# Experts' loop: order of a unit's three row stores, of the split of w1 and of the last transpositions in small units

## The chip, the cores and the metric

One core of a Trainium2 chip runs the whole program in one launch. The metric is the device time of that launch in microseconds (us), the median of three runs; a profiled execution of the same program gives the trace.

## The reference, cut to what matters

```python
attn = softmax(scale * q @ pool8(k).T) @ pool8(v)      # 8 x 8 heads, 576 x 64
x = attn.transpose(0, 2, 1, 3).reshape(4608, 512)

do = x @ w_skip > 0                       # tokens that go through an expert
e = argmax(x[do] @ w_gate); gate = softmax(x[do] @ w_gate)[e]
x[do] += gate * (relu(x[do] @ w1[e]) @ w2[e])          # 8 experts, 512 -> 1024 -> 512

h = x @ w_in; out = (h * sigmoid(h)) @ w_out           # 512 -> 2048 -> 512
```

The change touches the third stage, the experts. How many tokens an expert gets is known only at run time.

## The kernel before, in words

The program has three stages one after the other: attention (to about 160 us in the trace), the experts (about 160 to 507 us), and the last network. All products are made of three matmuls on split operands (high times high, high times low, low times high), so every operand is split into a high half (ScalarE, a copy to the shorter type) and a low half (VectorE, a subtraction).

**Units.** The tokens after attention lie in DRAM as rows of 520 floats, tensor `xa`: 512 values and 8 logits. Routing has made a table of token numbers by expert. The work is cut into units of up to three tiles of 128 tokens of one expert. The first unit is written out; then a loop, `tc.For_i`, line 1025, runs over the rest but one; the last unit is written out again behind the loop, among work of the next stage. The loop ran ten times here. Each pass reads the unit's number of tokens `n` and its columns of the table from `ut` into registers of every engine, and takes one of three arms: up to 256 rows (small), 320, or 384. 320 is 256 rows and a half tile (`mm2_half`, 64 rows).

**One pass** (lines 1026 to 1046) in the kernel before:

- SP loads the next unit's w1 (`load_w1`, 828, 2 MB in four parts) into `raw1`. `keep` (859) copies this unit's tokens from `xn` to `xr` on ScalarE and VectorE. GpSimd then gathers the next unit's rows from `xa` to `xn` (`gather`, 672, three indirect transfers) and stores tiles 1 and 0 of the unit before from `y` to `xa` (`scatter`, 882, one indirect transfer each).
- `mm1` (863): the first layer, eight blocks of twelve matmuls; each block's result is evicted and split into `hh`, `hl`, and a slice of w2 is split (`w2h`, `w2l`).
- `xtrans` (679) transposes the next unit's tokens on TensorE, two of four 128-column slices at a time, into two PSUM buffers; ScalarE and VectorE split them into `xth`, `xtl`, which the next pass's first layer reads.
- `gates` (891): the gate's weight `gt` from the logits, five small operations on VectorE and an exponential on ScalarE.
- `s2`, `gi`, `si`: small VectorE operations that make the row numbers of tile 2, of the gather after next and of tiles 0 and 1 from the table. In the trace `s2` is named `sq`, as it lies in the same tile.
- `conv1` (841): the split of the next unit's w1, four times; only then may SP load `raw1` again.
- `mm2` (906): the second layer of one tile, 24 matmuls, and a VectorE operation that writes `y` (named `x` in the trace).

In the small arm the order is `mm1`, first transpositions, gates, `s2` (`arm`, 978), then `unit_end` (994): store of tile 2, `gi`, `conv1`, `mm2` of tile 1 (left out when n is at most 128), last transpositions, `mm2` of tile 0, `si`. In the big arms `mm2` of the third tile comes between the first transpositions and `unit_end`.

**What sets the order.** Every engine executes its instructions in the order of the program text: the class `Ordered` records each one, and all have the line of its call, 117. What waits for what follows from the tiles read and written. `xa` is one tensor, so a gather waits for all stores before it, a store for the gather before it and for earlier stores, unless `declare_no_dep` says that two don't touch the same rows. `y`, `gi`, `si` and `s2` have one buffer each. SP runs ahead of the other engines until a load's buffer isn't free.

```python
                self.gather(gi)
                scatter(1)
                scatter(0)
```

Of the kernel before, what the change touches and what calls it, by code (L numbers as in the profile page):

```python
# [37 lines left out]
U = 3  # L38
# [121 lines left out]
class Kern:  # L160
# [686 lines left out]
    def moe(self, xa, up):  # L847
        nc, tc, c = self.nc, self.tc, self.c
        with tc.tile_pool(name="ms", bufs=1) as s1, \
# [13 lines left out]
            def mm1(n, fs=range(8), conv=True):  # L863
                for f in fs:
                    ps = self.hp.tile([P, DM], F32, name=f"hp{f}_{n}", tag="hp")
                    i = 0
                    for w, x in ((self.w1h, xth), (self.w1h, xtl), (self.w1l, xth)):
                        for k in range(4):
                            nc.tensor.matmul(ps[:, 0:n], w[:, k, P * f:P * (f + 1)], x[:, k, 0:n],
                                             start=(i == 0), stop=(i == 11))  # L870
                            i += 1
                    if n == 2 * P + D:
                        self.split(hh[:, f, 0:2 * P], hl[:, f, 0:2 * P], ps[:, 0:2 * P], relu=True)
                        nc.scalar.activation(hx[:, f], ps[:, 2 * P:n], AF.Relu)
                    else:
                        self.split(hh[:, f, 0:n], hl[:, f, 0:n], ps[:, 0:n], relu=True)
                    if conv:
                        self.conv2(raw2, f)
                    else:
                        nc.scalar.copy(self.w2h[:, f], raw2[:, f])  # L880

            def scatter(s, other=None, si=si):

                ids = self.s2 if s == 2 and si is self.si else si[:, s:s + 1]
                ins = nc.gpsimd.indirect_dma_start(xa, bass.IndirectOffsetOnAxis(ap=ids, axis=0), y[:, s],
                                                   None, bounds_check=NT - 1, oob_is_err=False)
                if other:
                    tc.declare_no_dep(ins.ins, other.ins, reason="disjoint rows")
                return ins

            def gates(gt=None):
                L = xr[:, :, DM:XW]
                v = nc.vector
                mx = s2.tile([P, U], F32, name="gmx", tag="gmx")
                v.tensor_reduce(mx, L, AX.X, ALU.max)
                d = s2.tile([P, U, E], F32, name="gd", tag="gd")
                v.tensor_tensor(d, L, bc(mx, 2, E), ALU.subtract)
                nc.scalar.activation(d, d, AF.Exp)
                if gt is None:
                    gt = s2.tile([P, U], F32, name="gt", tag="gt")  # L900
                v.tensor_reduce(gt, d, AX.X, ALU.add)
                v.tensor_scalar(gt, gt, 1e-9, None, ALU.add)
                v.reciprocal(gt, gt)
                return gt

            def mm2(s, gt, between=None):
                ps = (pp if s else self.hp).tile([P, DM], F32, name=f"yp{s}", tag="yp" if s else "hp")
                i = 0
                for f in range(8):
                    if between and f == 4:  # L910
                        between()
                    for h, w in ((hh, self.w2h), (hh, self.w2l), (hl, self.w2h)):
                        nc.tensor.matmul(ps, h[:, f, P * s:P * (s + 1)], w[:, f], start=(i == 0), stop=(i == 23))
                        i += 1
                nc.vector.scalar_tensor_tensor(y[:, s, 0:DM], ps, gt[:, s:s + 1], xr[:, s, 0:DM], ALU.mult, ALU.add)

            def mm2_half(gt):
                ps = pp.tile([P, DM], F32, name="yq", tag="yp")
                for f in range(8):
                    o = D * (f % 2)  # L920
                    nc.tensor.matmul(ps[o:o + D], hx[:, f], raw2[:, f], start=(f < 2), stop=(f >= 6),
                                     skip_group_check=True)
                o = y[0:D, 2, 0:DM]
                nc.scalar.copy(o, ps[D:P])
                nc.vector.tensor_tensor(o, ps[0:D], o, ALU.add)
                nc.vector.scalar_tensor_tensor(o, o, gt[0:D, 2:3], xr[0:D, 2, 0:DM], ALU.mult, ALU.add)
# [34 lines left out]
            def first_unit(cols, nxt):  # L961
                gt = gates()
                nc.vector.tensor_scalar(self.s2, cols[:, U - 1:U], -1.0, None, ALU.add)
                self.ffn_abs(0, self.raw1[:, 0], self.raw1[:, 1])
                for _ in self.ffn_ops(0):
                    pass
                self.ffn_conv3(0)
                self.ffn_load(3)
                self.rows(gi, nxt)
                for s in (2, 1):  # L970
                    mm2(s, gt)
                    if s == 2:
                        scatter(s)
                        nc.vector.tensor_scalar(si[:, 0:U - 1], cols[:, 0:U - 1], -1.0, None, ALU.add)
                self.xtrans((0, 1))
                mm2(0, gt, lambda: self.xtrans((2, 3)))

            def arm(n, e, gt, ld):
                mm1(n)
                if n != 2 * P + D:  # L980
                    load2(e)
                if n == 2 * P:
                    self.xtrans((0, 1))
                gates(gt)
                nc.vector.tensor_scalar(self.s2, self.table[:, bass.ds(ld(3, 0, EMPTY), 1)], -1.0, None, ALU.add)
                if n > 2 * P:
                    if n == 2 * P + D:
                        mm2_half(gt)
                        load2(e)
                    self.xtrans((0, 1))  # L990
                    if n == U * P:
                        mm2(2, gt)

            def unit_end(n, ld, gt, often=False):
                scatter(2)
                cols = self.table[:, bass.ds(ld(1, 0, EMPTY), U - 1)]
                self.rows(gi, ld(1, 2, EMPTY))
                for i in range(4):
                    self.conv1(i)
                if often:  # L1000
                    mm2(1, gt)
                else:
                    with tc.If(n > P) as cmp:
                        nc.before(cmp)
                        mm2(1, gt)
                    nc.after(cmp)
                self.xtrans((2, 3))
                mm2(0, gt)
                nc.vector.tensor_scalar(si[:, 0:U - 1], cols[:, 0:U - 1], -1.0, None, ALU.add)

            entry = lambda i, j, hi, engines: nc.value(self.ut[0:1, i, j:j + 1], hi, engines)
            self.taken()
# [6 lines left out]
            first_unit(self.table[:, SLOTS:EMPTY], entry(1, 1, EMPTY, dve))  # L1019
            for s in (1, 0, 2):  # L1020
                nc.scalar.copy(y[:, s, DM:XW], xr[:, U - 1, DM:XW])
            cols = nc.value(self.qi[0:1, 0:1], EMPTY, dve)
            nc.vector.tensor_scalar(self.sq, self.table[:, bass.ds(cols, U)], -1.0, None, ALU.add)
            nu = nc.values_load(self.nu[0:1, 0:1], min_val=1, max_val=NU - 2)
            with tc.For_i(0, nu, 1, iteration_sync="reg_based") as u:
                ld = lambda i, o, hi: nc.value(self.ut[0:1, i, bass.ds(u + o, 1)], hi)
                e = ld(0, 1, E - 1)
                self.load_w1(e)
                keep()
                n = ld(2, 0, U * P)  # L1030
                self.gather(gi)
                scatter(1)
                scatter(0)
                gt = s2.tile([P, U], F32, name="gt", tag="gt")
                with tc.If(n <= 256) as cmp:
                    arm(256, e, gt, ld)
                    unit_end(n, ld, gt)
                    nc.after(None)
                with cmp.Else():
                    with tc.If(n <= 320) as cmp2:  # L1040
                        arm(320, e, gt, ld)
                    with cmp2.Else():
                        arm(384, e, gt, ld)
                    nc.after(cmp2)
                    unit_end(n, ld, gt, True)
                nc.after(cmp)

            keep()
            scatter(1)
            scatter(0)  # L1050
            b0 = ORDER[0]
            x = self.raw1[:, 0:2].rearrange("p a (b n) -> p (a b) n", n=P)
# [16 lines left out]
            gt = gates()  # L1069
            one = s1.tile([1, 1], F32, name="one", tag="one")  # L1070
            nc.scalar.activation(one, gt[0:1, 0:1], AF.Silu)
            sc = None

            for k in range(5):
                if k < 4:
# [3 lines left out]

            for s in (2, 1):  # L1080
                mm2(s, gt)
                sc = scatter(s, sc, self.sq)
                while done:
                    f = done.pop(0)
                    self.ffn_conv3(f)
                    self.ffn_load(f + 3)
                some(OPS[6 - s])
            mm2(0, gt)
            scatter(0, None, self.sq)
            some(20)  # L1090
            while done:
                f = done.pop(0)
# [831 lines left out]
```

## Time and profile before

| | us |
|---|---|
| three runs | 1238.49, 1238.7, 1235.39 |
| median | 1238.49 |
| profiled execution, its own time | 1240.01 |
| span of its trace | 1238.2 |
| TensorE busy (matmul) | 1194.8, 96% of the span |
| VectorE, ScalarE, GpSimd busy | 937.1, 617.4, 398.1 |
| experts' loop, first unit's first product to the loop's exit | 188.77 to 472.19 |

A window row gives a stretch's length, then the busy time of each engine in it with the number of instructions, TensorE's granted clock (1.00 is 2.4 GHz), the DMA engines' share and their GB/s. A timeline row gives the start, the length, the engine, the instruction with output and inputs, and in brackets the engine's idle time before it with what ended it. "issue" means that the engine waited for nothing that the profile shows. Matmuls overlap, so lengths of single ones add up to more than the time they take.

### The profile page before, as it was taken

How to read it: one execution, taken by the hardware profiler on the slowest of the kernel's cores; microseconds unless marked ns; L12 is line 12 of the kernel's file. 1: busy time of each engine (PE TensorE's matmuls, PEld its weight loads, DVE VectorE, ACT ScalarE, POOL GpSimd, SP SyncE). 2: the span in 40 equal slices, each digit the busy share in tenths (PEclk: the TensorE clock that was granted, in tenths of full speed). 3: DMA queues.
4: the chain of work that ended last, by engine and by line, in shares of the span. 5: the costliest groups of instructions: out<-in, count | busy, mean ns of one | idle time of the engine just before them, and what ended most of it. 6: DMA issues, size and time to landing. Idle time of an engine off the chain costs nothing.

```text
span 1238.2 us, 20329 instructions
## 1 busy us (share of the span) xinstructions
PE 1194.8 (96%) x6173; PEld 1013.6 (82%) x6174; DVE 937.1 (76%) x1572; ACT 617.4 (50%) x1286; POOL 398.1 (32%) x345
## 2 busy tenths in 40 slices
PE   6999898999989999999999999999999999999997
PEld 5988787988878888888888888888888788887885
DVE  5888886566675768989668855767897778977667
ACT  5877534445564555444444334554355543555442
POOL 5477532222232221323357733222112221112210
PEclk9999999999999999999999999999999999999999
DMA  9997537465574753458849783677757786575645
GB/s 373 327 310 269 185 125 280 138 228 177 182 238 139 250 187 89 133 177 245 279 130 321 225 245 112 210 207 210 236 179 228 215 236 230 180 234 184 195 168 144
DMA packets 162767, 260.68 MB, mean 211 GB/s; under 512 B 41669, under 2 KB 91461, under 8 KB 160000
## 3 DMA queue, kind: packets, MB, share of 16 engines
q1 hardware_dynamic: 150880, 241.39, 60.5%
q0 software_dynamic: 7008, 16.80, 4.2%
q10 hardware_dynamic: 4800, 1.51, 0.5%
q8 instruction: 41, 0.67, 0.2%
q14 instruction: 38, 0.31, 0.1%
HBM read 203.16 MB, written 59.18 MB: 212 GB/s over the span
## 4 chain that ended last, share of the span: by engine, by line
PE 53%; DVE 4%; DMA 2%; POOL 1%; issue 1%; ACT 1%; SPq 0%; ACTq 0%; POOLq 0%; DVEq 0%
PE ps L117 17%; PE fopy L117 16%; PE fh L117 9%; PE fop L117 9%; PE yp L117 1%; DMA wout<-wdo 1%; DVE sw L117 1%; POOL sw L117 1%; DVE accc L117 1%; DMA ft<-part 1%; DMA wdi<-fh 0%; DMA wdo<-fl 0%; DVE fr L117 0%; DVE oc L117 0%; DVE c L117 0%
## 5 line engine op out<-in xcount | busy, mean ns | idle before, releaser
L117 PE MATMUL fopy<-c,wout 128*128 128x512 f32 x810 | 192.1, 391 | 2.2 <-DVE accc L117 2.0
L117 PEld LDWEIGHTS fopy<-c,wout 128*128 128x128 f32 x810 | 151.2, 188 | 37.0 <-DVE accc L117 5.0
L117 POOL TENSOR_TENSOR tm<-tm,tm 128x512 f32<-128x512 f32 x24 | 31.8, 1324 | 271.7 <-ACT tm L117 271.7
L117 DVE TENSOR_TENSOR accc<-fopy,accc 128x1024 f32<-128x1024 f32 (+1 forms) x73 | 87.9, 1205 | 23.0 <-PE fopy L117 23.0
L117 ACT ACTIVATE hh<-hp 128x256 fp32r<-128x256 f32 (+1 forms) x96 | 39.4, 410 | 97.7 <-PE hp L117 87.0
L117 DVE TENSOR_TENSOR w2l<-raw,w2h 128x512 fp32r<-128x512 f32 x96 | 65.8, 690 | 28.9 <-ACT w2h L117 26.3
L117 ACT CAST c<-hs 128x512 fp32r<-128x512 f32 x96 | 59.7, 622 | 55.1 <-PE fopy L117 28.0
L117 DVE TENSOR_TENSOR c<-hs,c 128x512 fp32r<-128x512 f32 x96 | 66.0, 688 | 23.6 <-ACT c L117 23.6
L117 POOL TENSOR_TENSOR sw<-sw 128x256 f32<-128x256 f32 x64 | 72.4, 1153 | 35.8 <-DVE sw L117 34.6
L117 PE MATMUL yp<-w2l,hh 128*128 128x512 f32 x208 | 81.7, 393 | 2.0 <-DVE w2l L117 2.0
L117 PE MATMUL yp<-w2h,hh 128*128 128x512 f32 x208 | 83.5, 402 | 0.0
L117 ACT COPY tm<-ps 128x512 f32<-128x512 f32 x72 | 42.0, 583 | 82.9 <-PE ps L117 82.9
L117 PE MATMUL fh<-w1l,fh 128*128 128x512 f32 x336 | 83.0, 389 | 0.0
L117 PE MATMUL yp<-w2h,hl 128*128 128x512 f32 x208 | 81.6, 392 | 0.0
L117 PE MATMUL hp<-xth,w1h 128*128 128x256 f32 (+2 forms) x384 | 72.0, 309 | 6.1 <-issue 2.8
L117 ACT ACTIVATE fsg<-fh 128x512 f32<-128x512 f32 x48 | 28.7, 597 | 92.6 <-PE fh L117 88.3
L117 PE MATMUL hp<-xtl,w1h 128*128 128x256 f32 (+2 forms) x384 | 71.7, 307 | 3.1 <-DVE xtl L117 1.9
L117 PEld LDWEIGHTS fh<-w1l,fh 128*128 128x128 f32 x336 | 63.1, 188 | 13.1
L117 DVE TENSOR_TENSOR fgl<-fsg,fgh 128x512 fp32r<-128x512 f32 x48 | 39.1, 816 | 41.5 <-ACT fgh L117 41.5
L117 ACT ACTIVATE prb<-s,mx 128x72 f32<-128x72 f32 x288 | 65.3, 355 | 10.3 <-DVE mx L117 10.3
L117 PE MATMUL hp<-xth,w1l 128*128 128x256 f32 (+2 forms) x384 | 70.0, 304 | 0.0
L117 PEld LDWEIGHTS hp<-xth,w1h 128*128 128x128 f32 x384 | 59.5, 189 | 9.4 <-issue 6.4
(252 smaller groups left out, 2952.4 us busy)
## 6 DMA issues: line engine op xcount, KB each, us to landing
raw<-w SPq DMA_DIRECT2D x88, 512.0 KB
wout<-wdo SPq DMA_DIRECT2D x135, 256.0 KB
win<-wdi SPq DMA_DIRECT2D x36, 512.0 KB
w1l<-wdi SPq DMA_DIRECT2D x36, 512.0 KB
xa<-x SPq DMA_DIRECT2D x36, 256.0 KB
v<-vR SPq DMA_DIRECT2D x7, 1280.0 KB
w1l<-wdo SPq DMA_DIRECT2D x33, 256.0 KB
fr<-w_in SPq DMA_DIRECT2D x16, 512.0 KB
```

What stands on the lines that cost most here:

```text
L117: ins = f(*a, **k)
```

## The change

- `scatter` takes a list of other stores that it need not wait for. A pass begins with the store of tile 0 alone; the stores of tile 2 and tile 1 both stand in the unit itself and are declared free of the earlier ones of the list. Tile 1's store comes after its `mm2`; a one-element GpSimd copy from `y` to a new tile `seen` stands before it. `si` is made before `mm2` of tile 1 instead of at the end.
- The small arm is a function of its own, `small`: `mm1`, w2's load, first transpositions, `s2`, store of tile 2, `conv1`, gates, `gi`, `si`, `mm2` of tile 1 if n is over 128, copy and store of tile 1, `mm2` of tile 0 with the last transpositions between its first and second half.
- The big arms keep their order but for `si` and the store of tile 1.
- The first unit stores its tile 1 itself; behind the loop one store is left; the last unit's list holds all its earlier stores.

```diff
--- before.py
+++ after.py
@@ -879,13 +879,13 @@
                     else:
                         nc.scalar.copy(self.w2h[:, f], raw2[:, f])
 
-            def scatter(s, other=None, si=si):
+            def scatter(s, others=(), si=si):
 
                 ids = self.s2 if s == 2 and si is self.si else si[:, s:s + 1]
                 ins = nc.gpsimd.indirect_dma_start(xa, bass.IndirectOffsetOnAxis(ap=ids, axis=0), y[:, s],
                                                    None, bounds_check=NT - 1, oob_is_err=False)
-                if other:
-                    tc.declare_no_dep(ins.ins, other.ins, reason="disjoint rows")
+                for o in others:
+                    tc.declare_no_dep(ins.ins, o.ins, reason="disjoint rows")
                 return ins
 
             def gates(gt=None):
@@ -970,43 +970,60 @@
                 for s in (2, 1):
                     mm2(s, gt)
                     if s == 2:
-                        scatter(s)
+                        last = scatter(s)
                         nc.vector.tensor_scalar(si[:, 0:U - 1], cols[:, 0:U - 1], -1.0, None, ALU.add)
+                    else:
+                        scatter(s, [last])
                 self.xtrans((0, 1))
                 mm2(0, gt, lambda: self.xtrans((2, 3)))
 
+            seen = s1.tile([1, 1], F32, name="seen", tag="seen")
+
+            def small(n, e, gt, ld, sc):
+                mm1(2 * P)
+                load2(e)
+                self.xtrans((0, 1))
+                nc.vector.tensor_scalar(self.s2, self.table[:, bass.ds(ld(3, 0, EMPTY), 1)], -1.0, None, ALU.add)
+                sc.append(scatter(2, sc))
+                cols = self.table[:, bass.ds(ld(1, 0, EMPTY), U - 1)]
+                for i in range(4):
+                    self.conv1(i)
+                gates(gt)
+                self.rows(gi, ld(1, 2, EMPTY))
+                nc.vector.tensor_scalar(si[:, 0:U - 1], cols[:, 0:U - 1], -1.0, None, ALU.add)
+                with tc.If(n > P) as cmp:
+                    nc.before(cmp)
+                    mm2(1, gt)
+                nc.after(cmp)
+                nc.gpsimd.tensor_copy(seen, y[0:1, 1, 0:1])
+                scatter(1, sc)
+                mm2(0, gt, lambda: self.xtrans((2, 3)))
+
             def arm(n, e, gt, ld):
                 mm1(n)
-                if n != 2 * P + D:
+                if n == U * P:
                     load2(e)
-                if n == 2 * P:
-                    self.xtrans((0, 1))
                 gates(gt)
                 nc.vector.tensor_scalar(self.s2, self.table[:, bass.ds(ld(3, 0, EMPTY), 1)], -1.0, None, ALU.add)
-                if n > 2 * P:
-                    if n == 2 * P + D:
-                        mm2_half(gt)
-                        load2(e)
-                    self.xtrans((0, 1))
-                    if n == U * P:
-                        mm2(2, gt)
-
-            def unit_end(n, ld, gt, often=False):
-                scatter(2)
+                if n < U * P:
+                    mm2_half(gt)
+                    load2(e)
+                self.xtrans((0, 1))
+                if n == U * P:
+                    mm2(2, gt)
+
+            def unit_end(ld, gt, sc):
+                sc.append(scatter(2, sc))
                 cols = self.table[:, bass.ds(ld(1, 0, EMPTY), U - 1)]
                 self.rows(gi, ld(1, 2, EMPTY))
                 for i in range(4):
                     self.conv1(i)
-                if often:
-                    mm2(1, gt)
-                else:
-                    with tc.If(n > P) as cmp:
-                        nc.before(cmp)
-                        mm2(1, gt)
-                    nc.after(cmp)
+                nc.vector.tensor_scalar(si[:, 0:U - 1], cols[:, 0:U - 1], -1.0, None, ALU.add)
+                mm2(1, gt)
+                nc.gpsimd.tensor_copy(seen, y[0:1, 1, 0:1])
+                scatter(1, sc)
                 self.xtrans((2, 3))
                 mm2(0, gt)
-                nc.vector.tensor_scalar(si[:, 0:U - 1], cols[:, 0:U - 1], -1.0, None, ALU.add)
 
             entry = lambda i, j, hi, engines: nc.value(self.ut[0:1, i, j:j + 1], hi, engines)
             self.taken()
@@ -1019,6 +1036,7 @@
             first_unit(self.table[:, SLOTS:EMPTY], entry(1, 1, EMPTY, dve))
             for s in (1, 0, 2):
                 nc.scalar.copy(y[:, s, DM:XW], xr[:, U - 1, DM:XW])
+            nc.scalar.copy(seen, xr[0:1, U - 1, 0:1])
             cols = nc.value(self.qi[0:1, 0:1], EMPTY, dve)
             nc.vector.tensor_scalar(self.sq, self.table[:, bass.ds(cols, U)], -1.0, None, ALU.add)
             nu = nc.values_load(self.nu[0:1, 0:1], min_val=1, max_val=NU - 2)
@@ -1029,12 +1047,10 @@
                 keep()
                 n = ld(2, 0, U * P)
                 self.gather(gi)
-                scatter(1)
-                scatter(0)
+                sc = [scatter(0)]
                 gt = s2.tile([P, U], F32, name="gt", tag="gt")
                 with tc.If(n <= 256) as cmp:
-                    arm(256, e, gt, ld)
-                    unit_end(n, ld, gt)
+                    small(n, e, gt, ld, sc)
                     nc.after(None)
                 with cmp.Else():
                     with tc.If(n <= 320) as cmp2:
@@ -1042,11 +1058,10 @@
                     with cmp2.Else():
                         arm(384, e, gt, ld)
                     nc.after(cmp2)
-                    unit_end(n, ld, gt, True)
+                    unit_end(ld, gt, sc)
                 nc.after(cmp)
 
             keep()
-            scatter(1)
             scatter(0)
             b0 = ORDER[0]
             x = self.raw1[:, 0:2].rearrange("p a (b n) -> p (a b) n", n=P)
@@ -1069,7 +1084,7 @@
             gt = gates()
             one = s1.tile([1, 1], F32, name="one", tag="one")
             nc.scalar.activation(one, gt[0:1, 0:1], AF.Silu)
-            sc = None
+            sc = []
 
             for k in range(5):
                 if k < 4:
@@ -1079,14 +1094,14 @@
 
             for s in (2, 1):
                 mm2(s, gt)
-                sc = scatter(s, sc, self.sq)
+                sc.append(scatter(s, sc, self.sq))
                 while done:
                     f = done.pop(0)
                     self.ffn_conv3(f)
                     self.ffn_load(f + 3)
                 some(OPS[6 - s])
             mm2(0, gt)
-            scatter(0, None, self.sq)
+            scatter(0, (), self.sq)
             some(20)
             while done:
                 f = done.pop(0)
```

## Rows read from the trace of the kernel before

**Rows 1.** The page's first part: busy time of each engine, share of the span, instructions.

```profile
PE 1194.8 (96%) x6173; PEld 1013.6 (82%) x6174; DVE 937.1 (76%) x1572; ACT 617.4 (50%) x1286; POOL 398.1 (32%) x345
```

**Rows 2.** Windows, one per unit: length; busy PE, PEld, DVE, ACT, POOL; PEclk, DMA share, GB/s.

```profile
188.77:216.26 27.49, 24.35 (x157) 21.61 (x157) 18.07 (x35) 13.82 (x27) 6.00 (x5) 0.99 0.86 307
216.26:252.36 36.10, 36.10 (x181) 33.13 (x181) 19.64 (x36) 14.35 (x26) 7.09 (x7) 0.96 0.49 163
...
276.24:306.31 30.07, 30.07 (x173) 25.38 (x172) 19.60 (x37) 15.39 (x35) 8.35 (x7) 1.00 0.60 205
...
336.38:356.42 20.04, 18.44 (x133) 17.09 (x132) 15.30 (x31) 13.29 (x26) 6.33 (x5) 1.00 0.55 175
356.42:386.70 30.28, 26.07 (x158) 22.96 (x156) 21.55 (x39) 13.70 (x26) 8.08 (x7) 0.94 0.68 233
...
416.77:440.34 23.57, 23.57 (x158) 21.59 (x157) 18.70 (x35) 13.29 (x26) 7.10 (x6) 1.00 0.64 214
```

**Rows 3.** TensorE's timeline: start, length, instruction, count, idle time before it and its releaser.

```profile
216.26 1.62 PE L117 MATMUL hp<-xth,w1h 128*128 128x384 f32 x4 [2.75 <-issue]
...
347.69 0.82 PE L117 MATMUL xtp<-ident,xn 128*128 128x128 f32 x6
...
350.11 1.01 PE L117 MATMUL xtp<-ident,xn 128*128 128x128 f32 x6 [1.60 <-DVE xtl L117]
...
359.18 0.82 PE L117 MATMUL hp<-xtl,w1h 128*128 128x256 f32 x2 [1.89 <-DVE xtl L117]
...
370.21 0.27 PE L117 MATMUL xtp<-ident,xn 128*128 128x128 f32 x1
...
373.02 1.11 PE L117 MATMUL xtp<-ident,xn 128*128 128x128 f32 x4 [1.16 <-DMA xn<-xa,gi]
...
472.19 0.94 PE L117 MATMUL hp<-xth,w1h 128*128 128x384 f32 x4 [1.62 <-PEq L1920]
```

**Rows 4.** Windows around the turn to unit 1 and the loop's exit, columns as above.

```profile
213.00:216.00 3.00, 0.50 (x3) 0.08 (x1) 0.46 (x2) 0.00 (x0) 0.00 (x0) 0.97 1.02 409
216.00:217.00 1.00, 0.74 (x2) 0.77 (x3) 0.56 (x2) 0.00 (x0) 0.64 (x1) 0.50 0.45 172
...
472.00:474.00 2.00, 1.81 (x10) 1.84 (x11) 1.32 (x3) 1.71 (x2) 0.97 (x1) 1.00 0.03 8
```

**Rows 5.** GpSimd's timeline in the loop, units 4 to 6.

```profile
321.02 1.01 POOL L117 DMA_INDIRECT xa<-x,si  x1 [2.64 <-DMA xa<-x,si]
...
339.20 1.42 POOL L117 DMA_INDIRECT xn<-xa,gi  x1 [8.88 <-PE hp L117]
...
348.12 1.02 POOL L117 DMA_INDIRECT xa<-x,si  x1 [4.75 <-DMA xn<-xa,gi]
...
353.99 1.75 POOL L117 DMA_INDIRECT xa<-x,si  x1 [4.85 <-DMA xa<-x,si]
...
364.44 1.50 POOL L117 DMA_INDIRECT xn<-xa,gi  x1 [3.06 <-PE hp L117]
...
376.85 1.00 POOL L117 DMA_INDIRECT xa<-x,si  x1 [1.96 <-DMA xa<-x,si]
```

**Rows 6.** VectorE's timeline, end of unit 4.

```profile
332.79 0.75 DVE L117 SCALAR_TENSOR_TENSOR x<-yp,gt,xr 128x512 f32<-128x512 f32 x1
```

**Rows 7.** VectorE's timeline, turn from unit 0 to unit 1.

```profile
219.54 0.70 DVE L117 COPY xr<-xn 128x1040 f32<-128x1040 f32 x1 [2.98 <-issue]
```

**Rows 8.** VectorE's and ScalarE's timelines, unit 5.

```profile
350.43 0.17 DVE L117 TENSOR_REDUCE gmx<-xr 128x3 f32<-128x24 f32 x1
...
353.44 0.17 DVE L117 TENSOR_SCALAR gi<-table 128x3 int32 x1 [1.06 <-issue]
353.63 4.63 DVE L117 TENSOR_TENSOR w1l<-raw,w1h 128x1024 fp32r<-128x1024 f32 x4
...
355.00 0.85 ACT L117 CAST xth<-xtp 128x384 fp32r<-128x384 f32 x2
...
358.48 1.02 DVE L117 TENSOR_TENSOR xtl<-xtp,xth 128x384 fp32r<-128x384 f32 x2 [0.22 <-DVEq L1003]
```

## The prediction

> **What bounds the kernel now.** I read the page first: TensorE is busy for 96% of the span and no other engine comes near [rows 1]. So a store or a transposition that moves is worth only what it takes from TensorE's idle time or from its slow-clock time. I then cut the experts' loop into its ten units, from the first matrix product of one to that of the next, and asked for the busy time in each [rows 2]. I number them 0 to 9. Units 3, 4 and 7 take the 320-row arm and last 30.07 us each, without a gap. Unit 8, a small unit (256-row arm) with both second products, lasts 23.57 us without a gap. Against these the loss stands in few places: unit 0 lasts 27.49 us and holds 24.35 us of work; unit 5, a small unit with a single second product, has 1.6 us of idle time; unit 6, of the same kind as unit 8, takes 30.28 us instead of 23.57. That is 6.7 us in unit 6 alone.
>
> TensorE's timeline names the waits [rows 3]: 1.60 us in unit 5 before the second pair of transpositions, which needs the PSUM buffers of the first; 1.89 us early in unit 6 for the low half of the transposed tokens (`xtl`); 1.16 us, the second of two waits, for the gathered tokens (`xn`); 2.75 us between units 0 and 1 for nothing the profile shows. The granted clock tells the rest: unit 5 ran at 1.00 in spite of its wait, but after the gap before unit 1 the clock fell to 0.50, that is 1.2 instead of 2.4 GHz, and unit 6's mean is 0.94 [rows 2, 4].
>
> **Part 1: stores that don't wait for each other, the second inside its unit.** Now a unit's chain on GpSimd is gather, store 1, store 0, store 2, each held until the one before has landed, and then the next gather [rows 5]. In unit 5 store 1 goes at 348.12, store 0 at 353.99, and store 2 so late that the gather of unit 6 starts at 364.44, after 3.06 us of waiting. Its last tokens are waited for until 373.02, so a gather takes 8.6 us there. After the change store 0 comes first, store 2 waits for no store, and store 1 is the last in its unit; the next gather waits for store 1 instead of store 2. Nothing but this gather is queued behind store 1 on GpSimd. Each store still costs one issue of about 1 us; none is added.
>
> In unit 5 store 1 must wait for its row numbers `si`, which part 2 puts at 358.4; a start near 359.3 allows 0.9 us for the hand-over. How long it holds the gather no row shows. The nearest are store to store: 2.98 us (an issue of 1.02 and a wait of 1.96, before 376.85; it is this very store, all of whose rows are dropped), 3.65 us (before 321.02) and 5.87 us (before 353.99, beside weight loads) [rows 5]. I take 2.98, as unit 5 has at most 128 rows and its store 1 drops them all: 362.3. VectorE's copy of the old tokens, which must also come first, ends at about the same time, so 362.6: 1.8 us earlier than now, and the tokens land near 371.2. The end kept for the range is 5.87.
>
> In the other small units the wait could grow. Unit 5's own gather follows unit 4, whose second product is written at 332.79 for 0.75 us [rows 6]. With `si` ahead of it and a one-element copy on GpSimd behind it, store 1 starts near 334.6, and at 3.65 us the gather could go at 338.3, before it does now (339.20). At 5.87 us it is 340.5, 1.3 us late, of which about 0.4 is covered: the store that waits for all its tokens goes at 348.12, and TensorE turned to them at 347.69 [rows 3, 5]. Units 0, 2 and 8 are given the same ends, 0 and 0.9 us less what they have in hand. I take 0.3 us of loss in all four; the ends are 0 and 2.5. The one-element copy has no row; between nothing and the 1 us of a store's issue it delays the same gather and lies within these ends.
>
> The Trainium skill's page "DMA: Bandwidth & Descriptors" (section "Anatomy of one DMA — SWDGE (gpsimd) path") fits 2.0 us plus the bytes over 436 kB per us, an estimate of 2.6 us for a store of 128 rows of 2080 bytes. By it no gather would be late and the 0.3 us would be 0. The rows show 2.98 to 5.87, so they decide.
>
> **Part 2: w1's split ahead of the gates, in small units.** In unit 5 VectorE has now the gates from 350.43, a register read and `s2`, two reads (1.06 us) and `gi`, the four splits for 4.63 us from 353.63, and `xtl` of the second pair from 358.48 [rows 8]. After: `s2` (one read of 0.53 and 0.15) to 351.1, a read, the splits to 356.3, the gates (1.27) to 357.5, a read, `gi` and `si` (0.17 each) to 358.4, `xtl` from 358.6. No work goes; the low half is ready 0.15 us later than now. On ScalarE the high halves `xth`, copied at 355.00 now, stand behind the gates' exponential, which then waits for the splits: about 356.9, the first ready at 357.4. The loads of w1 are released 2.5 us sooner on SP's queue; TensorE waits for none of them. In big units only `si` is new ahead of the second product's write, 0.17 us, under 3 us of product: nothing.
>
> **Part 3: the last transpositions amid a product.** Unit 8's rest after the first layer is 23.57 - 11.31 = 12.26 us (the layer is unit 5's, 336.38 to 347.69); the same work after the change. With T the end of the layer, `xtl` is there at T + 12.6 (10.9 as in unit 5, and the second product's write and the splitting, 1.76) against a need at T + 13.2, six matmuls into the next layer: nothing lost; end for the range 0.3 us a unit, within the 2.5 above. In unit 5 the 1.60 us wait goes, since the buffers are free by the middle of the product, and TensorE is done at about 354.5 instead of 356.42. But the next layer's third matmul needs `xth` (357.4) and its seventh `xtl` (359.3): the two waits become one of 2.8 us and one near 1.1, and the layer resumes where it does now. The row nearest to a wait of 2.8 us is the one of 2.75: half clock. Unit 1 shows the price, a mean clock of 0.96 over 36.10 us: 1.4 us [rows 2]. The Trainium skill ("TensorE: Matmul & The Clock Gate", part 1) has the same in kind: an idle TensorE is throttled to half rate. By the waits of 1.60 and 1.89 us alone there would be no loss.
>
> **Sum.** Unit 6's layer, which ends at 370.21 now, ends at 370.21 + 0.15 + 1.4 = 371.8; the tokens are there (371.2); the rest takes 12.26 at full clock: 384.0 instead of 386.70, a gain of 2.7. Its ends: full clock, the tokens deciding, 3.2; a late store and a half clock, a loss of 0.8. Less 0.3 for late gathers: 2.4 us. The 2.75 us gap and its half clock stay: VectorE had a gap of 2.98 us at the same turn, ending at 219.54, with the DMA engines hardly loaded any more (share 0.45 from 216 on), and both waited for nothing the profile shows [rows 3, 4, 7]. The other reading, that first entry into other code is delayed by weight loads (DMA share 1.02 then), would bring it down to the 1.62 us of the loop's exit, where the share was 0.03 and the clock full [rows 3, 4]: 1.1 + 1.4 = 2.5 us, kept for the range. After the loop one store fewer stands before the token loads; TensorE doesn't wait for those: nothing.
>
> Profiled execution: 1240.01 - 2.4 = 1237.6 us. It lies 1.5 us above the median of the runs, 1238.49; against that: **1236.1 us**.
>
> **Rivals.** *The gap before unit 1 shrinks too.* For: weight loads end some 2.5 us sooner, before the turn. Against: VectorE's gap with little DMA. Time: 1236.1 - 2.5 = 1233.6. *The in-unit store becomes the new wait.* It stands before every gather, and the gathers of five small units (0, 2, 5, 6, 8) are nearly just in time. At 5.87 us from store to gather this takes 2.5 + 0.8 and the gain: 1241.8, and each further us adds up to 5; slower by more than a measurement can tell from about 6 us on, 1244 at 6.4. Against: 3.65 where weight loads don't interfere. *The wait only changes its name.* Unit 6's gather is held by store 1 as long as by store 2 now, and the clock takes the rest: 1238.5.
>
> **How the numbers follow.** Forecast 0.48, shrinking gap 0.26, no net change 0.14, new wait 0.12. About 0.3%, 3.7 us, is what a measurement can tell from no change. Faster: nearly all of the second case and the upper quarter of the forecast's spread, 0.37. Slower: nearly all of the last, 0.11. Same: the rest, 0.52. The range reaches from both gains with unit 6's best, 1238.5 - 5.7, to the new wait at 5.87 us: 1232.8 to 1241.8.
>
> **What would show it.** Right: unit 6 near 28 us with no wait for `xn`; unit 5 shorter by 2 us; one long wait for `xth` between them and a clock of 0.5 after it; the gap before unit 1 unchanged; units 3, 4 and 7 at 30.07. Wrong: waits for `xn` in units 0, 2 or 8 (the new wait); full clock early in unit 6, or a gap under 2 us before unit 1 (more gain); unit 6 still near 30 us (no gain).

## The result: 0.64% slower, and the profile after

| | before | after |
|---|---|---|
| median of 7 runs of each | 1237.63 us | 1244.29 us |
| lowest to highest | 1235.39 to 1242.65 | 1243.83 to 1247.85 |
| profiled execution, its own time | 1240.01 | 1244.0 |
| span of its trace | 1238.2 | 1242.2 |

The ratio is 1.0064, 95% interval 1.0048 to 1.0081. I had forecast 1236.1 us with a range up to 1241.8: wrong in sign, and outside the range. By "store 1" I mean the store of tile 1, and so on for 0 and 2. TensorE's work is the same; its busy time rose by 1.8 us [rows 1], the span by 4.0. The page's first part, after:

```profile
PE 1196.6 (96%) x6173; PEld 1015.1 (82%) x6174; DVE 939.7 (76%) x1572; ACT 617.8 (50%) x1287; POOL 399.7 (32%) x355
```

The windows of units 0, 1, 3, 5, 6 and 8, after (columns as in [rows 2]):

```profile
189.26:217.53 28.27, 25.99 (x156) 23.61 (x157) 18.13 (x34) 14.04 (x27) 6.84 (x7) 0.91 0.74 243
217.53:253.69 36.16, 36.16 (x180) 33.08 (x181) 19.46 (x35) 14.36 (x27) 6.26 (x7) 0.95 0.54 182
277.35:307.43 30.08, 30.08 (x173) 25.47 (x172) 19.49 (x37) 15.37 (x35) 8.49 (x8) 1.00 0.62 206
337.51:356.19 18.68, 18.40 (x133) 17.11 (x132) 15.40 (x25) 11.69 (x22) 5.86 (x5) 1.00 0.62 208
356.19:388.83 32.64, 26.62 (x158) 22.77 (x156) 21.80 (x45) 15.21 (x30) 8.52 (x9) 0.95 0.59 199
418.90:442.47 23.57, 23.57 (x158) 21.59 (x156) 18.88 (x35) 13.40 (x26) 6.11 (x7) 1.00 0.58 191
```

Against [rows 2]: units 3 and 8 are the same to 0.01 us, unit 1 to 0.06, unit 5 is 1.36 us shorter, unit 6 is 2.36 us longer, unit 0 0.78 us longer. One loss lies in no unit's window. From the last half product of the first unit (the second half of its last `mm2`, ahead of the loop) to the loop's first matmul TensorE took 3.60 us before (185.17 to 188.77) and takes 7.76 now (181.50 to 189.26). ScalarE and TensorE there, before:

```profile
185.88 0.40 ACT L117 COPY x<-xr 128x8 f32<-128x8 f32 x3
...
188.77 1.02 PE L117 MATMUL hp<-xth,w1h 128*128 128x256 f32 x4 [0.62 <-DVEq L1025]
```

The timelines of GpSimd, ScalarE and TensorE there, after:

```profile
183.24 1.00 POOL L117 DMA_INDIRECT xa<-x,si  x1 [0.17 <-issue]
189.05 1.04 POOL L117 DMA_INDIRECT xn<-xa,gi  x1 [4.81 <-DMA xa<-x,si]
...
188.38 0.39 ACT L117 COPY x<-xr 128x8 f32<-128x8 f32 x3 [6.06 <-DMA xa<-x,si]
188.68 0.18 ACT L117 COPY seen<-xr 1x1 f32<-1x1 f32 x1
...
189.26 1.33 PE L117 MATMUL hp<-xth,w1h 128*128 128x256 f32 x4 [4.76 <-ACTq L1043]
```

The first unit's store 1 is the new part of the change that I had passed over. It is issued at 183.24. ScalarE's next work is the filling of `y`'s logits columns, tile 1 first: it writes what that store still reads, so it waits 6.06 us for the store to land (before there was no such store, and no wait). ScalarE then enters the loop late, and TensorE waits at the entry for ScalarE's queue (line 1043 is the loop), 4.76 us. The first layer of unit 0 then starts at half clock, as the window 189 to 194 shows:

```profile
189.00:194.00 5.00, 4.74 (x21) 4.71 (x22) 1.08 (x2) 1.52 (x3) 3.07 (x3) 0.50 0.77 270
```

In unit 6 the next gather now comes behind unit 5's store 1. GpSimd and TensorE, after:

```profile
360.19 0.99 POOL L117 DMA_INDIRECT xa<-x,si  x1 [0.56 <-issue]
366.89 1.25 POOL L117 DMA_INDIRECT xn<-xa,gi  x1 [5.71 <-PE hp L117]
...
358.38 0.74 PE L117 MATMUL hp<-xth,w1h 128*128 128x256 f32 x2 [1.79 <-ACT xth L117]
360.15 0.82 PE L117 MATMUL hp<-xtl,w1h 128*128 128x256 f32 x2 [0.76 <-DVE xtl L117]
371.93 0.30 PE L117 MATMUL xtp<-ident,xn 128*128 128x128 f32 x1 [0.96 <-DMA xn<-xa,gi]
372.67 0.33 PE L117 MATMUL xtp<-ident,xn 128*128 128x128 f32 x1 [0.44 <-DMA xn<-xa,gi]
374.89 0.66 PE L117 MATMUL xtp<-ident,xn 128*128 128x128 f32 x4 [1.90 <-DMA xn<-xa,gi]
```

The store goes at 360.19 and the gather 6.70 us later, 10.7 us into the unit; before it was 8.0 us into it (364.44 - 356.42) [rows 2, 5]; in a second profile of each kernel (experiment 6) it is 10.4 and 6.8. The row names a matmul as what ended the gather's wait, but the layer's matmuls end all the time there; the store had landed 0.8 us before (5.9 us after its issue), and experiment 4 takes its wait away. TensorE waits 3.30 us for tokens, against 2.21 (1.05 and 1.16) before [rows 3 has the second].

So there are two candidates: the entry wait (theory A) and the gathers behind in-unit stores (theory B). A single profile can't rank them, because the same code ahead of the loop ends anywhere from 163.3 to 171.7 us in the profiles of this study. I therefore compare the medians and the **loop stretch**: from the first matmul of the first unit's second layer, ahead of the loop (167.48 in before), to the first matmul behind the loop, the last unit's (472.19). The row of 188.77 to 472.19 in the table of before is shorter, as it begins at unit 0, behind the entry.

| kernel | loop stretch of the profile | median | ratio to before |
|---|---|---|---|
| before; once more | 304.7; 300.6 | 1236.9 to 1237.6 | |
| after; once more | 310.6; 310.6 | 1244.29 | 1.0064 [1.0048, 1.0081] |
| copy of tile 1 ahead | 312.9 | 1243.69 | 1.0048 [1.0031, 1.0065] |
| before, store 1 in the first unit | 307.7 | 1241.3 | 1.0031 [1.0019, 1.0044] |
| after, no store 1 in the first unit | 305.9 | 1241.66 | 1.0036 [1.0021, 1.0050] |
| after, store 1 where nobody waits | 301.8 | 1236.77 | 1.0004 [0.9985, 1.0024] |
| after, store 1 in the next unit | 300.8 | 1237.23 | 1.0008 [0.9993, 1.0023] |
| before, independent stores only | 303.7 | 1238.34 | 1.0003 [0.9988, 1.0017] |
| store 1 in the next unit, transpositions ahead | 298.4; 301.3 | 1235.29 | 0.9976 [0.9956, 0.9996] |
| the same, low half read last | 298.5 | 1233.7 | 0.9970 [0.9950, 0.9990] |

### The profile page after: what moved, and what is told of

The parts are those of the page before. It is cut to its first block, busy times and chain, and to the rows that moved or that the text cites. A ratio compares the mean times of both kernels' runs of the same rounds, so it can differ in the third digit from the quotient of the medians.

```text
span 1242.2 us, 20360 instructions
## 1 busy us (share of the span) xinstructions
PE 1196.6 (96%) x6173; PEld 1015.1 (82%) x6174; DVE 939.7 (76%) x1572; ACT 617.8 (50%) x1287; POOL 399.7 (32%) x355
## 4 chain that ended last, share of the span: by engine, by line
PE 56%; DVE 3%; issue 1%; DMA 0%; ACT 0%; POOL 0%; ACTq 0%; POOLq 0%; DVEq 0%
PE ps L117 17%; PE fopy L117 17%; PE fh L117 10%; PE fop L117 10%; PE yp L117 1%; DVE accc L117 1%; DMA wout<-wdo 0%; DVE fr L117 0%; DVE sw L117 0%; DVE oc L117 0%; DVE c L117 0%; DVE raw L117 0%; ACT c L117 0%; ACTq L117 0%; DVE w2l L117 0%
```

## The experiments

**1. Is the entry wait the loss?** One copy moves, nothing else:

```diff
+            nc.scalar.copy(y[:, 1, DM:XW], xr[:, U - 1, DM:XW])
             first_unit(self.table[:, SLOTS:EMPTY], entry(1, 1, EMPTY, dve))
-            for s in (1, 0, 2):
+            for s in (0, 2):
```

> The changed kernel with one ScalarE copy moved: the logits columns of y's tile 1 are filled ahead of the first unit, so that nothing on ScalarE has to wait for the first unit's new store 1. Theory A (the loss is made at the loop's entry: the copy waits for that store to land, ScalarE enters the loop late, TensorE waits for it 4.76 us and then runs at half clock): the time from the first unit's last half product to the loop's first matmul goes from 7.76 us back to about 3.6, unit 0's first layer from 13.55 to 12.2 us, and the whole falls by 4.2 + 1.3 = 5.5 us, to about 1238.8 (ratio to before 1.001). Theory B (the loss is that the in-unit store holds every next gather): the entry gap may shrink, but the program stays near 1244, since waits for the gathered tokens are what cost.

Measured: the entry is 3.60 us again and the first layer 11.64 us, as theory A says, and yet the median is 1243.69, which the spread of the runs does not tell from 1244.29. So the 5.5 us that theory A put on the entry wait don't come back. What stood under the entry wait shows in GpSimd's and TensorE's timelines of this kernel:

```profile
185.96 1.00 POOL L117 DMA_INDIRECT xa<-x,si  x1 [0.17 <-issue]
193.02 1.04 POOL L117 DMA_INDIRECT xn<-xa,gi  x1 [6.05 <-PE hp L117]
...
200.69 0.33 PE L117 MATMUL xtp<-ident,xn 128*128 128x128 f32 x1 [0.90 <-DMA xn<-xa,gi]
202.35 0.66 PE L117 MATMUL xtp<-ident,xn 128*128 128x128 f32 x4 [1.33 <-DMA xn<-xa,gi]
```

The same store also stands before unit 0's gather, which now starts 5.2 us into the unit (193.02 - 187.85) instead of 2.7 (191.50 - 188.77). TensorE waits 2.23 us for tokens (0 to 1.39 in the kernels without that store), and the clock's mean falls to 0.62 from 202 to 206. In the changed kernel the entry wait had covered that: its gather was out (189.05) before unit 0 began. One store has two queues behind it; freeing one exposes the other. (In this profile the gap before unit 1 was 5.01 us too, against 2.0 to 3.6 in all others but one; its own time, 1248.82, is the highest of its six.)

**2. The first unit's store alone.** Added to the kernel before:

```diff
                     if s == 2:
-                        scatter(s)
+                        last = scatter(s)
                         nc.vector.tensor_scalar(...)
+                    else:
+                        scatter(s, last)
```

> The kernel before with one store added and nothing else: store 1 of the first unit also goes inside the first unit (its rows are stored once more by the loop's first pass). Theory A: the entry wait appears by itself, TensorE idles about 4.2 us more there and unit 0 loses about 1.3 us to the half clock: 1237.6 + 5.5 = 1243. Theory B: the in-unit stores of the loop are not there, so no loss: 1237.6, at most 1 us more for the added store.

Measured: 1241.3, that is 3.8 us more (0.0031 x 1236.9; 2.3 to 5.4). The entry wait came by itself (5.67 us, from ScalarE's queue, 8.65 us from half product to loop), with half clock behind it.

**3. The loop's in-unit stores alone.** The rest of the change stays:

```diff
-                    else:
-                        scatter(s, [last])
```

> The changed kernel without the first unit's store 1 (those rows of the first expert are never added: work is left out); the in-unit stores of the loop stay. It has no entry wait, and the gather of unit 0 stands behind store 2 alone. If the first unit's store is responsible for what adding it to the kernel before cost (4.4 us, half of it by holding the copies or the gather of unit 0), the time falls from 1244 to about 1239.5, and what is left over before (about 2 us) is the loop's own in-unit stores: unit 6 stays at 32 us. If the loop's stores were the whole loss, it stays at 1243 to 1244; if they cost nothing, it reaches 1237.

Measured: 1241.66, by the ratio 4.4 us more than before (2.6 to 6.2); the entry took 3.62 us, unit 6 31.90. So the first unit's store and the loop's stores cost about the same: 3.8 and 4.4 make 8.2, where the whole change has 7.9 by its ratio (0.0064 x 1237.6; 5.9 to 10.0). The loop's share is about twice what I expected here.

**4. The wait or the traffic?** Store 1 is aimed at a second DRAM tensor, with the copy of experiment 1 ahead:

```diff
-                ins = nc.gpsimd.indirect_dma_start(xa, ...
+                ins = nc.gpsimd.indirect_dma_start(self.xd if s == 1 and si is self.si else xa, ...
```

> The changed kernel with the copy of tile 1's logits moved ahead, and every store 1 of the experts' loop and of the first unit sent to another DRAM tensor of the same shape, which nobody reads (so its rows are missing from the result). The stores go at the same places with the same bytes, but no gather and no copy waits for one. Theory B (what costs is the wait of the next gather for store 1 to land): unit 0 loses its 3 us of waits for tokens, unit 6 falls from 32 to about 28.5 us, the time to 1237. Rival (what costs is the store's traffic and its issue on GpSimd, not the wait): 1243 to 1244 as now.

Measured: 1236.77, as before. The stores are all there at the same places, and that of unit 5 takes 5.6 us to land, much as after (5.9); only nobody waits. GpSimd in unit 6 of this kernel:

```profile
354.68 0.98 POOL L117 DMA_INDIRECT xd<-x,si  x1 [0.63 <-issue]
357.30 1.35 POOL L117 DMA_INDIRECT xn<-xa,gi  x1 [1.64 <-PE hp L117]
```

2.62 us from store to gather instead of 6.70, and no wait for tokens in unit 6. The loss is the wait for store 1 to land, by whoever has to wait: shown for the gathers and the copy together, and by experiments 2 and 3 for the two places.

**5. What the rest of the change is worth.** Store 1 goes back behind the next unit's gather (store 0 waits for it, as before); and, from the other side, the kernel before gets independence of store 2 alone.

```diff
-                sc = [scatter(0)]
+                sc = [scatter(1), scatter(0)]
...
-                nc.gpsimd.tensor_copy(seen, y[0:1, 1, 0:1])
-                scatter(1, sc)
```

and from the kernel before:

```diff
-                scatter(1)
-                scatter(0)
+                sc = [scatter(1), scatter(0)]
...
-                scatter(2)
+                scatter(2, sc)
```

> The changed kernel with store 1 put back behind the next unit's gather (and so none in the first unit); store 2 still waits for neither of the other stores, w1 is still split ahead of the gates in small units, the last transpositions still stand amid the product. It has neither the entry wait nor an in-unit store before the gather. Theory A: the same as the changed kernel with the copy moved, about 1238.8. Theory B with A: below that one by what late gathers cost, 1 to 1.5 us (unit 6 falls from 32.64 to about 30 us or less), so 1237 to 1238. My first reasoning about half clock and earlier gathers, if it holds at all here, would give 1236.

> The kernel before with one part of the change: store 2 of a unit waits for neither store 0 nor store 1 (the order of the stores and all else as before). In unit 5 store 2 can go as soon as its data is there, so the gather of unit 6 (364.44 in before) starts up to 2 us sooner. If that gather alone is what makes unit 6 slow (30.28 us against 23.57 in unit 8), the time falls by 1 to 3 us, to 1235 to 1236.5; if unit 6 is held by the splitting (xth, xtl) as well, the wait only changes its name: 1237.6.

Measured: 1.0008 and 1.0003: neither can be told from before. Units 5 and 6 take 47.13 and 47.35 us together. Against the profile of before (50.32) both look like a gain of 3 us; the next run shows why it is none.

**6. The two kernels once more.**

> The kernel before, once more, for the spread of its units from run to run: if units 0 and 6 come out at 27.49 and 30.28 us again, those are its own times and the other kernels' differ by their edits; if unit 6 is nearer 27.5, as in the kernel before with a store added (27.64, the same code there), the 30.28 was one run's.

> The changed kernel once more, for the same: the entry gap of 7.8 us and a unit 6 of 32 to 33 us should be there again if they are the kernel's own; a unit 6 below 30 us would say that its 32.64 was one run's.

Measured: before 1235.51, after 1244.55. Units 5 and 6 of before now, and of after, then the window around 357 us in before, from their windows:

```profile
331.70:351.74 20.04, 18.44 (x134) 17.09 (x132) 15.31 (x31) 13.29 (x26) 5.89 (x6) 1.00 0.59 196
351.74:379.28 27.54, 25.54 (x158) 22.99 (x156) 21.50 (x39) 13.39 (x26) 8.69 (x7) 0.94 0.68 224
...
356.30:358.30 2.00, 2.00 (x11) 2.00 (x11) 1.12 (x2) 0.89 (x2) 0.00 (x0) 0.50 0.85 330
```

```profile
341.37:360.06 18.69, 18.41 (x134) 17.11 (x132) 15.38 (x25) 11.69 (x22) 5.88 (x5) 1.00 0.59 203
360.06:390.36 30.30, 26.19 (x158) 23.07 (x156) 21.72 (x45) 15.21 (x30) 8.22 (x9) 0.94 0.60 202
```

Unit 6 of before takes 27.54 us, 2.7 less than in the profile that I had worked from, and has no wait for tokens. In experiments 2 and 5 (the two built on the kernel before) it took 27.64 and 27.29. The 30.28 us was one run's, though its place is real: the tokens there have little in hand. After, units 5 and 6 take 51.32 and 48.99, before 50.32 and 47.58: 1.0 and 1.4 us more each time. The entry gap is there again, 9.39 us. Its unit 6 waits for tokens in both profiles (3.30 us, then 1.38); that of before in one of two.

**7. The order inside small units.** Both start from the kernel with store 1 in the next unit; one puts the gates ahead of w1's splitting again, the other the last transpositions ahead of the last product.

```diff
-                for i in range(4):
-                    self.conv1(i)
                 gates(gt)
                 self.rows(gi, ld(1, 2, EMPTY))
+                for i in range(4):
+                    self.conv1(i)
```

```diff
-                mm2(0, gt, lambda: self.xtrans((2, 3)))
+                self.xtrans((2, 3))
+                mm2(0, gt)
```

> The kernel with store 1 put back in the next unit, and in small units the gates ahead of w1's splitting again (as in the kernel before). If the new order only shifts which wait ends last, unit 6's wait for xth (1.85 us) goes and the wait for xtl behind it takes all of it (about 2.7 us), and units 5 and 6 together stay within 0.3 us of the 47.13 us with the splitting first. If the order gains something, the sum of the two rises by 0.5 us or more. If a single wait of 2.7 us does what the gap of 2.75 us before unit 1 did, the granted clock falls to 0.50 behind it and unit 6 rises by 1.4 us.

> The kernel with store 1 put back in the next unit, and in small units the last transpositions ahead of the last product again (as in the kernel before). Unit 5 gets its wait of 1.60 us back (20.0 us instead of 18.69) and unit 6 loses the wait for xth, keeping 1.0 to 1.9 us for xtl: the sum of both stays near 47.1 to 47.6 us if the wait only changed its name, and rises to 48.5 us if the move alone was worth its 1.35 us.

Each ran once, profiled, in 1244.69 and 1239.7 us, where one run of before took 1241.09: too few for the times to tell. Gates first: units 5 and 6 take 48.06 us; the wait for `xth` fell to 0.76, that for `xtl` rose to 1.62, 2.38 in all against 2.68, and half clock lasted some 7 us. The wait did move, but not wholly, and the sum rose through the clock: inconclusive on the order. Transpositions ahead: 45.79 us, a miss low by 1.3. The wait of 1.60 in unit 5 is back, those in unit 6 are 0.37 and 0.83, and this time no half clock followed:

```profile
338.84:358.90 20.06, 18.46 (x133) 17.09 (x132) 16.41 (x28) 11.91 (x23) 8.07 (x6) 1.00 0.59 193
358.90:384.63 25.73, 24.40 (x157) 21.57 (x156) 19.95 (x42) 14.70 (x29) 7.95 (x7) 1.00 0.67 226
```

**8. Two versions a little faster than both.** The last kernel timed, and with one more edit in the first layer:

```diff
-                    for w, x in ((self.w1h, xth), (self.w1h, xtl), (self.w1l, xth)):
+                    for w, x in ((self.w1h, xth), (self.w1l, xth), (self.w1h, xtl)):
```

> The same kernel as the one with the last transpositions ahead of the last product, now timed: its single look had units 5 and 6 at 45.79 us together, with full clock throughout, against 47.13 to 47.70 in the kernels whose TensorE waits 1.85 us or more at the start of unit 6. If that is the kernel's own (waits of 1.60, 0.37 and 0.83 us don't cost the clock, one of 1.9 does), it is faster than before by 1 to 2 us, ratio 0.9985 to 0.999, and unit 6 is below 26 us again. If the full clock was one run's luck, unit 6 is near 27.5 us and the ratio 1.000.

> The same, and in each group of 12 matmuls of the first layer the four that read the low half of the tokens come last instead of in the middle, so that TensorE needs xtl four matmuls (0.4 to 0.5 us at 256 columns) later at a unit's start; the low half of w1, which then comes sooner, is ready well before. The wait of 0.83 us for xtl in unit 6 falls to about 0.4; all else as in the one before: 0.4 us less, too little for the times to tell, so the trace's waits decide. If the low half of w1 is late instead, a new wait for w1l shows at the start of a small unit and the time doesn't fall.

Measured: 1235.29 and 1233.7, ratios 0.9976 and 0.9970, both with intervals below 1, the first by little (0.9996). The full clock was luck: in its second profile the first kernel had half clock after waits of 0.51 and 0.88 us, and unit 6 took 27.55. With the low half last the wait for `xtl` is 0.37 us, as expected, and TensorE's timeline has no other new wait at unit 6:

```profile
351.55 0.74 PE L117 MATMUL hp<-xth,w1h 128*128 128x256 f32 x2 [0.56 <-ACT xth L117]
353.37 0.82 PE L117 MATMUL hp<-xtl,w1h 128*128 128x256 f32 x2 [0.37 <-DVE xtl L117]
```

Why they gain is not settled. Shorter waits that cost the clock more seldom in unit 6 would fit, but two profiles of one and one of the other show no rate. The timed profiles are also of the slowest of the first kernel's twelve runs (1239.15) and the fastest of the second's (1229.52), and the intervals of the two overlap, as the first's does with that of the kernel it is built on (0.9993 to 1.0023). What they keep of the change is the independent store 2, the earlier `si` and w1's split ahead of the gates; they drop the in-unit store 1 and the transpositions amid the product.

## Why the prediction was wrong, point by point

- **"Nothing but this gather is queued behind store 1 on GpSimd."** True of GpSimd, and the step that failed: I asked only who is queued behind the store on its own engine, not who writes its source on another. The first unit's store 1 got no step of its own, only "0 and 0.9 us" for unit 0. ScalarE's copy waited 6.06 us for it, and TensorE for ScalarE. That place costs 3.8 us (experiment 2). With the copy out of the way unit 0's gather has the wait instead (experiment 1), at a price that no run gives by itself.
- **"I take 2.98" from store 1 to the gather, ends to 5.87.** Mis-sized. From issue to issue it was 6.70 us in unit 5, 6.42 in the second profile, and 7.06 ahead of unit 0 in experiment 1. Unit 5's store 1 itself went as predicted: at 360.19, where unit 5 starts 1.13 us later than in before, against 359.3. Only its landing was wrong, and so the gather went at 366.89 instead of 362.6, 3.2 us more than that shift; TensorE waited for tokens until 374.89, where the sum had them there at 371.2. The DMA view after, of 359 to 368 us, has it from the other side (operation, count, KB each, us from issue to landing):

```profile
raw<-w SPq DMA_DIRECT2D x4, 512.0 KB, 5.6
xa<-x,si POOLq DMA_INDIRECT x1, 5.9
```

  5.9 us to land, beside four weight loads. I had called 2.98 "this very store", but it was measured at 376.85, at another point of the unit; the row beside weight loads, 5.87 [rows 5], was the near one. That this store drops all its rows, my reason for the short figure, did not help: it moved 0.00 MB and still took 5.9.

  The first unit issues two stores that drop no rows, 0.27 MB each (128 rows of 2080 bytes). The DMA views of the kernel of experiment 1 show them, store 2 of 182.2 to 185.9 us and store 1 of 185.9 to 193 (a queue's row: packets, MB, share of the engines):

```profile
q0 software_dynamic: 80, 0.27, 18.9%
xa<-x,sq POOLq DMA_INDIRECT x1, 2.8
...
q1 hardware_dynamic: 857, 1.75, 70.6%
q0 software_dynamic: 80, 0.27, 9.2%
xa<-x,si POOLq DMA_INDIRECT x1, 6.3
```

  Store 2, with no other transfer moving beside it, landed in 2.8 us; store 1, beside loads of 1.75 MB, in 6.3. The Trainium skill's fit ("DMA: Bandwidth & Descriptors", section "Anatomy of one DMA — SWDGE (gpsimd) path") would make a store of 128 rows an estimate of 2.6 us. The trace agrees for store 2 and disagrees for store 1.
- **The gain of 2.7 us in unit 6.** It was taken from 30.28 us in one profiled run. In the three other profiles of that kernel and of those built on it the unit takes 27.3 to 27.6, so most of what I meant to win was not there to be won.
- **Half clock after one long wait, none after 1.60 and 1.89.** Wrong as a rule. The second profile of before has half clock behind those same waits (0.50 at 356.3 to 358.3); the profile after has full clock behind 1.79 and 0.76.
- **The rival "the in-unit store becomes the new wait"** came true: it named 1244 us, slower from about 6 us on; measured were 1244.29 and 6.70. The mechanism stood in the text with a chance of 0.12. That the time agrees is partly chance: the rival's 1244 was for the loop's gathers alone, and these cost 4.4 us (1241.66 without the first unit's store); the rest came from the entry, which it did not have. Nor do the five small units share the loss, as it says: in both profiles after only unit 6 waits for tokens, units 2, 5 and 8 don't, though unit 5's gather too went later (341.11, 3.6 us into the unit; 2.8 before). Those gathers had more in hand than I read.
- **Right:** in unit 5 ScalarE's second `xth` at 356.9 and VectorE's second `xtl` from 358.6 predicted, 357.75 and 359.44 measured, in a trace where the unit starts 1.13 us later, so both to 0.3 us; the wait of 1.60 us in unit 5 gone, the unit shorter (2 us predicted, 1.36 measured); a wait for `xth` and one for `xtl` in its place (2.8 and 1.1 predicted, 1.79 and 0.76 measured); the gap before unit 1 in the same place (2.28 us, half clock behind it); units 3, 4 and 7 unchanged.

## What to carry to other kernels

When a store moves earlier, list for its source every later writer on every engine, and for its target every later reader, and price each with the landing time measured at that place of the loop, not with the shortest row of the same kind. Here ScalarE's 6.06 us at the loop's entry became 4.76 us of TensorE, the engine that bounds the kernel. Before a forecast rests on a stretch of a few us, look whether a second profile, or the other units of the same kind, shows it as well.

## What the runs showed of the hardware that I had not expected

The granted clock after an idle stretch is not fixed by its length. Before unit 1 the clock stayed at 1.00 after 3.02 us of idle time (before, once more) and 2.08 us (low half last), and fell to about 0.5 after 2.75 (before) and 2.71 us (transpositions ahead, second profile). Unit 1 took 34.55, 34.60, 36.10 and 35.95 us in these four, so the same code may differ by 1.5 us by the clock alone. The Trainium skill ("TensorE: Matmul & The Clock Gate", part 1) says that an idle TensorE is throttled to half rate. The traces agree that it happens after idle stretches, and show besides that it doesn't happen after each.

A store of the same 0.27 MB landed in 2.8 us alone and in 6.3 beside weight loads, and one that dropped all its rows still took 5.9 beside such loads.
